# Where two kinds of weight stores stand in the transfers' queue, in a kernel of windowed attention and a Fourier-mixed feed-forward layer

## The chip, the cores and the metric

The kernel runs on one core of a Trainium2 chip. Such a core has TensorE (PE; the profile shows its weight loads apart as PEld), VectorE (DVE), ScalarE (ACT), GpSimd (POOL) and SyncE (SP). Each engine works through its own instructions in order, and SP does nothing here but issue transfers between the off-chip memory (DRAM) and on-chip memory. A transfer that has to wait for data or for a buffer holds SP until it can go, and with it all transfers that stand behind. The metric is the device time of one execution in microseconds (us); several runs are taken and their median compared.

## What is computed

Two layers, one after the other, for 4 sequences of 768 positions.

```python
# attention: 8 heads of 64, a window of 128 positions and 4 sink positions
keep = is_sink | in_window
scores = np.where(keep, scale * q @ k.T, -1e9)
x = softmax(scores) @ v                       # (4, 768, 512)
# Fourier mixing and feed-forward
u = x + real(fft(fft(x, axis=1), axis=2))
un = (u - mean(u)) / sqrt(var(u) + 1e-6)
out = u + relu(un @ w_ch1) @ w_ch2            # w_ch1 512 x 2048, w_ch2 2048 x 512
```

The weights arrive as 64-bit floating point numbers, two 32-bit words each, and everything is computed to the accuracy of 32-bit numbers, though products run on TensorE with rounded operands: each operand is split into a rounded high part and a low part, and three products (high by high, high by low, low by high) are added up.

## The kernel before

**Stages.** The 24 blocks of 128 positions form six groups of four (`groups`). Attention and the Fourier mixing run first, up to about 205 us. Then comes the feed-forward layer of group 0, in which the weights are also converted; it ends at about 333 us with the first product of group 1. Groups 1 to 5 use the converted weights; from line 1375 on, under `tc.manual_schedule()`, the order of the instructions is the written one. Before that line, and so in group 0's stage, the compiler's scheduler decides the order on each engine: it goes by the order of the program, but takes later work where an instruction would have to wait.

**The raw weights.** w1 (w_ch1) and w2 (w_ch2) come in 16 slices each. `W_ORDER` interleaves them: for each pair p of slices, places 4p and 4p+1 are two slices of w1, 4p+2 and 4p+3 two of w2, so there are 32 loads, numbered 0 to 31. `load_w(i)` issues load i (L599, 512 KB) into a tile with the tag "ld" that has three buffers (`LDB`). `convert(i)` turns the two words of each number into one 32-bit number by three DVE instructions (L614, L615, L616), then calls `load_w(i + 3)`, whose load needs the buffer that has just been read.

**The split.** A converted slice goes through an ACT cast for the high part and a POOL subtraction for the low part: L625 and L626 for w1, into one half of `w_ring` (two halves, one for each pair in turn), L639 and L640 for w2, into tiles that stay. PE needs both: `ch1` (L676) multiplies by w_ring, `ch2` (L1172) by the w2 tiles.

**The stores.** Later groups need w1 again, and with it sums and differences of its quarters, as they use a product scheme with seven instead of eight half-size products. So for each pair p two things are written to `w_dram[p]` in DRAM:

- the quarters (L629, 768 KB): three of the four in w_ring, issued in `convert(4p + 1)` after the POOL subtraction L626;
- the sums (L661, 1024 KB): `combine_w1(p)` forms four sums on POOL (L651 to L654) in a tile `tq`; the inner function `halves`, put off to the next slice by the list `late`, splits them by ACT casts (L659) and POOL subtractions (L660) into the tile `to`, and stores it. `tq` and `to` have one buffer each.

**The loop.** For each slice f of group 0 the loop at L1316 runs `ch1`, the relu (`split`, L1165 and L1166, tile h_sb), `ch2` of the slice before, the conversions of places 2f+4 and 2f+5, the `late` work and `combine_w1`. In the last slices it also prepares group 1 (`prepare_1`: L551, L552, L560, L1230, and the sums of the activations L1268, L1271, L1274). After the loop the tiles for the later stream of weights are set up: three of them take the buffers of the raw loads ("ld"), others those of `to`, `tq` and h_sb, and `load(n)` (L1364) reads `w_dram` back into them as w_c, w_t, w_q and w_h.

Of the kernel before, what the change touches and what calls it, by code (L numbers as in the profile page):

```python
# [205 lines left out]
def kernel(  # L206
# [14 lines left out]
    nc = tc.nc  # L221
    V, A, G, T = nc.vector, nc.scalar, nc.gpsimd, nc.tensor

    def f32(ap):
        return ap.bitcast(F32)
# [10 lines left out]
    w_dram = [dpool.tile([P, 7, 512], F32, name=f"wd{i}") for i in range(NPR)]  # L236
# [37 lines left out]
    def run(general):  # L274
        tag = "g" if general else ""
        with ExitStack() as p1:
# [314 lines left out]

            W_ORDER = [(w, 2 * p + j) for p in range(NPR) for w in range(2) for j in range(2)]

            def load_w(i):
                if i < 2 * NF:
                    which, f = W_ORDER[i]
                    r = npool.tile([P, 512, 2], I32, tag="ld", name=f"raw{i}", bufs=LDB)
                    src = w1i[f].rearrange("p c f -> p (c f)") if which == 0 else w2i[P * f:P * f + P]
                    nc.sync.dma_start(r.rearrange("p f t -> p (f t)"), src)  # L599
                    raw[i] = r  # L600

            def convert(i, pool=None):

                which, f = W_ORDER[i]
                r = raw.pop(i)
                if which == 0:
                    if f % 2 == 0:
                        state["tw"] = npool.tile([P, 2, 512], I32, tag="tw", name=f"tw{f}", bufs=1 if general else 2)
                    t = state["tw"][:, f % 2]
                else:  # L610
                    t = npool.tile([P, 512], I32, tag="qs0", name=f"cv{i}", bufs=QSB)

                w = state["h"].tile([P, 512], I32, tag="cw", name=f"cw{i}")
                V.tensor_scalar(w, r[:, :, 1], 3, 0x3FFFFFF8, op0=ALU.logical_shift_left, op1=ALU.bitwise_and)  # L614
                V.scalar_tensor_tensor(w, r[:, :, 1], -0x40000000, w, op0=ALU.bitwise_and, op1=ALU.bitwise_or)  # L615
                V.scalar_tensor_tensor(t, r[:, :, 0], 29, w, op0=ALU.logical_shift_right, op1=ALU.bitwise_or)  # L616
                load_w(i + LDB)
                tf = t.bitcast(F32)
                if which == 0:
                    if f == 0:  # L620
                        state["ring"] = npool.tile([P, 2, 4, 2, 256], F32R, tag="ring", name="w_ring", bufs=1)
                    fb = state["ring"][:, f // 2 % 2]
                    d = [fb[:, 0:2, j] if f % 2 == 0 else fb[:, 3:1:-1, j] for j in range(2)]
                    tf = tf.rearrange("p (h c) -> p h c", h=2)
                    A.copy(d[0], tf)  # L625
                    G.tensor_tensor(d[1], tf, f32(d[0]), op=ALU.subtract)  # L626
                    Wt[f, 0] = [[d[j][:, cc // 2, P * (cc % 2):P * (cc % 2) + P] for cc in range(NCC)] for j in range(2)]
                    if f % 2 == 1:
                        nc.sync.dma_start(w_dram[f // 2][:, 0:3], f32(fb[:, 0:3]).rearrange("p k s c -> p k (s c)"))  # L629
                        state["t", f // 2] = state["tw"].bitcast(F32)  # L630
                    return
                if NWA <= f < NWA + NHALF:

                    if f == NWA:
                        state["fold"] = [npool.tile([P, NHALF, DM], F32R, tag=t, name=f"w_{t}", bufs=1) for t in ("gh", "gl")]
                    d = [t[:, f - NWA] for t in state["fold"]]
                else:
                    d = [pool.tile([P, 512], F32R, name=f"w{f}_{j}") for j in range(2)]
                A.copy(d[0], tf)  # L639
                G.tensor_tensor(d[1], tf, f32(d[0]), op=ALU.subtract)  # L640
                Wt[f, 1] = d
# [3 lines left out]
            def combine_w1(p, pool):  # L645

                t = state.pop(("t", p))
                b11, b21, b12, b22 = t[:, 0, :256], t[:, 0, 256:], t[:, 1, :256], t[:, 1, 256:]
                q = pool.tile([P, 4, 256], F32, tag="tq", name=f"tq{p}")
                o = pool.tile([P, 4, 2, 256], F32R, tag="to", name=f"to{p}")  # L650
                G.tensor_tensor(q[:, 1], b12, b11, op=ALU.subtract)  # L651
                G.tensor_tensor(q[:, 0], b22, q[:, 1], op=ALU.subtract)
                G.tensor_tensor(q[:, 2], b22, b12, op=ALU.subtract)
                G.tensor_tensor(q[:, 3], b21, q[:, 0], op=ALU.subtract)  # L654

                def halves():
                    for j in (0, 2):
                        with tc.issue_after(state["relu"]):
                            A.copy(o[:, j:j + 2, 0], q[:, j:j + 2])  # L659
                        G.tensor_tensor(o[:, j:j + 2, 1], q[:, j:j + 2], f32(o[:, j:j + 2, 0]), op=ALU.subtract)  # L660
                    nc.sync.dma_start(w_dram[p][:, 3:7], f32(o).rearrange("p k s c -> p k (s c)"))  # L661

                late.append(halves)

# [15 lines left out]
            def start_ffn(s):  # L680
                state["h"] = p1.enter_context(tc.tile_pool(name="ps_h" + tag, bufs=1, space=PSUM))
                banks.append((p1.enter_context(tc.tile_pool(name="ps_n" + tag, bufs=1, space=PSUM)), "n", 1))
                for i in range(LDB):
                    load_w(i)
                for i in range(2):
                    at(s + CONV_AT[i], "V", lambda i=i: convert(i))
                for f in range(2):
                    at(s + CH1_AT[f], "T", lambda f=f: hp.append(ch1(0, f, unT0)))
# [458 lines left out]
            if general:  # L1147
# [4 lines left out]
                s = 0  # L1152
# [4 lines left out]
            else:  # L1157
                s = window_attention(fourier, load_constants)
# [155 lines left out]
            for i in (2, 3):  # L1314
                convert(i, wa)
            for f in range(NF):  # L1316
                ps = hp.pop(0) if f < 2 else ch1(0, f, unT0)
                hs[f] = g0.tile([P, 2, 512], F32R, tag="h", name=f"h_sb{f}", bufs=2)
                hs[f] = [hs[f][:, i] for i in range(2)]
                split(hs[f], ps)  # L1320
                if pw is None:
                    do(1)
                if f > 0:
                    ch2(f - 1, hs.pop(f - 1), po)
                for i in range(2 * f + 4, min(2 * f + 6, 2 * NF)):
                    if i % 2 and pw is None:
                        do(1)
                    if W_ORDER[i][0] == 1 and W_ORDER[i][1] == NWA + NHALF and pw is None:
                        while ev:
                            do(1)  # L1330
                        pf.close()
                        pf = None
                        pw = p1.enter_context(tc.tile_pool(name="wb" + tag, bufs=1))
                        state["x"] = [pw.tile([P, 7, 512], F32R, name=f"x{i}") for i in range(2)]
                        state["xf"] = pw.tile([P, 2, NCC, 256], F32, name="xf")
                    convert(i, wa if pw is None else pw)
                while late:
                    late.pop()()
                if f == 0 or f % 2 == 1 and f // 2 + 1 < NPR:
                    combine_w1((f + 1) // 2, g0)  # L1340
                if f == PREP:
                    steps = prepare_1()
                for _ in range(PREP_N if f >= PREP else 0):
                    next(steps, None)
            for _ in steps:
                pass
            while late:
                late.pop()()

            places = [npool.tile([P, 2, 2, 256], F32R, tag="ld", name=f"w1_c{i}", bufs=LDB) for i in range(LDB)]  # L1350

# [23 lines left out]
            with tc.manual_schedule():  # L1375
# [101 lines left out]
                for it in range(NIT):  # L1477
# [12 lines left out]
                    for k in range(7):  # L1490
                        if BANK.index(BANK[k]) == k:
                            pool, t = {"B": banks[it % 2][:2]}.get(BANK[k], (state["h"], {"A": "h", "C": "cw"}.get(BANK[k])))
# [4 lines left out]
                        a, b, c = (ps.get(x) for x in "ABC")  # L1497
# [102 lines left out]
                for g in range(2, len(groups)):  # L1600
# [7 lines left out]
                    ps, t, uh = {}, 0, {}  # L1608
                    for it in range(0, NIT, 2):
                        for k in range(7):  # L1610
                            for i in range(2):
                                c = it + i
# [4 lines left out]
                                p = ps[i, BANK[k]]  # L1617
# [37 lines left out]
                    for s2 in range(7 * NIT):  # L1655
                        k, c = divmod(s2, NIT)
                        if c == 0 and BANK.index(BANK[k]) == k:
                            ps[BANK[k]] = get(2, BANK[k], f"q{BANK[k]}_{g}")
                        p = ps[BANK[k]]
# [16 lines left out]
                        if g == 2 and 6 <= s2 < 6 + NPR:  # L1676
                            f = s2 - 6
                            for a in range(2):
                                nc.sync.dma_start(f32(Wt[2 * f, 1][a])[:, 256:], t_dram[f][:, 3, 256 * a:256 * a + 256])
                        do_x(xs, s2)  # L1680

    run(False)
    general = nc.values_load(outside[0:1, 0:1])
    with tc.If(general != 0):
        run(True)
# [77 lines left out]
```

## Time and profile before

| | us |
|---|---|
| median of 3 runs | 750.85 |
| lowest and highest run | 748.47, 751.24 |
| profiled execution, its own time | 752.84 |
| span of the profile, first to last instruction | 751.0 |
| PE busy in the span | 719.0 (96%) |
| DVE busy | 558.1 (74%) |
| ACT busy | 357.2 (48%) |
| POOL busy | 272.7 (36%), all of it before 430 us |
| mean granted TensorE clock | 0.988 |

The profile shows one execution. A row of instructions gives its start and duration, the engine, the line, the operation, the tiles it writes and reads, how many are merged into the row, and in square brackets how long the engine was idle before and what ended that. A row of waits gives who waited for whom, the total in us, how often, and the longest. Transfers appear at SP's issue; the time until the data has landed is listed apart.

### The profile page before, as it was taken

To read this page: it belongs to the slowest core of one execution; us is meant where nothing else is said; L and a number is where in the kernel's file an instruction comes from. 1 tells how busy PE (TensorE), PEld (TensorE's weight loads), DVE (VectorE), ACT (ScalarE), POOL (GpSimd) and SP (SyncE) were. 2 spreads that over 40 slices of the span, in tenths; PEclk is the share of its full clock that TensorE was granted. 3 is DMA by queue.
4 is the path that set the end of the run, shared out by engine and by line. 5 is a ranking of instruction groups with operands and counts; after the bars stand their busy time and mean duration, and the time that the engine had idled before them with its cause. 6 is when DMAs were issued, how large, how long until landed. Compare 5 with 4: busy or idle time off the path is not lost.

```text
span 751.0 us, 15699 instructions
## 1 busy us (share of the span) xinstructions
PE 719.0 (96%) x5539; PEld 644.0 (86%) x5539; DVE 558.1 (74%) x1299; ACT 357.2 (48%) x901; POOL 272.7 (36%) x391
## 2 busy tenths in 40 slices
PE   7999998999989999998999999999999999999996
PEld 5676876867868887687899999999999999999996
DVE  6678578888799888958677666957697578846772
ACT  4687666676633537423324144533444245523541
POOL 2467367478466898842995000000000000000000
PEclk9899999999999999999999999999999999999998
DMA  9754624533225898889999798879975897759831
GB/s 298 243 166 132 172 72 140 163 114 103 72 71 179 298 342 306 284 306 404 344 311 326 243 348 304 292 242 385 370 245 177 295 396 256 258 211 371 277 98 61
DMA packets 109576, 181.69 MB, mean 242 GB/s; under 512 B 9868, under 2 KB 44812, under 8 KB 108336
## 3 DMA queue, kind: packets, MB, share of 16 engines
q1 hardware_dynamic: 109200, 176.83, 69.2%
q0 software_dynamic: 288, 3.76, 1.3%
q8 instruction: 46, 0.75, 0.4%
q14 instruction: 42, 0.34, 0.1%
HBM read 148.04 MB, written 32.51 MB: 240 GB/s over the span
## 4 chain that ended last, share of the span: by engine, by line
PE 67%; DVE 14%; POOL 7%; issue 4%; ACT 4%; DMA 2%; SPq 1%; DVEq 0%; POOLq 0%; ACTq 0%
PE pB L1391 10%; PE qB L1568 9%; PE pA L1391 7%; PE pC L1391 6%; PE qC L1568 6%; PE qA L1568 6%; PE o L1419 5%; PE xt L854 4%; PE s L759 4%; PE pt L816 2%; PE za L398 1%; PE zb L398 1%; DVE sm L778 1%; POOL w_ring L626 1%; PE h L676 1%
## 5 line engine op out<-in xcount | busy, mean ns | idle before, releaser
L1590 ACT CAST hring<-x 128x512 fp32r<-128x512 f32 x92 | 57.0, 619 | 52.0 <-PE qB L1568 18.8
L784 ACT ACTIVATE sm<-sm,mx 128x132 f32<-128x132 f32 x192 | 75.9, 400 | 5.5 <-DVE mx L778 5.5
L1594 DVE TENSOR_TENSOR hring<-x,hring 128x512 fp32r<-128x512 f32 x92 | 63.4, 689 | 14.8 <-ACT hring L1590 9.6
L759 PE MATMUL s<-ring,q 64*128 64x260 f32 x320 | 50.8, 424 | 7.7 <-DVE mx L778 4.6
L778 DVE CUSTOM_DVE_ANT_0 sm<-s,mask 128x132 f32<-128x132 f32 x192 | 48.5, 293 | 7.1 <-PE s L757 1.7
L676 PE MATMUL h<-un_slots,w_ring 128*128 128x512 f32 x192 | 49.4, 404 | 2.1 <-POOL w_ring L626 1.5
L676 PEld LDWEIGHTS h<-un_slots,w_ring 128*128 128x128 f32 x192 | 36.3, 194 | 10.7 <-POOL w_ring L626 2.6
L759 PEld LDWEIGHTS s<-ring,q 64*128 64x128 f32 x320 | 27.9, 191 | 20.5 <-issue 6.7
L823 ACT COPY pta<-pt 128x512 f32<-128x512 f32 x48 | 28.1, 585 | 26.5 <-PE pt L816 26.4
L854 PE MATMUL xt<-ptl,ldv 128*64 128x128 f32 x384 | 40.2, 291 | 0.0
L1568 PE MATMUL qA<-w,hring 128*128 128x256 f32 x312 | 39.8, 279 | 0.0
L1419 PE MATMUL o<-w,hring 128*128 128x512 f32 x156 | 38.5, 393 | 1.3 <-ACT hring L1165 1.1
L1172 PE MATMUL o<-w,h_sb 128*128 128x512 f32 x156 | 38.3, 393 | 0.5 <-POOL w L640 0.5
L1568 PEld LDWEIGHTS qA<-w,hring 128*128 128x128 f32 x312 | 37.9, 189 | 0.0
L765 DVE COPY_PREDICATED s<-older,s 128x256 f32<-128x256 uint8 x80 | 33.7, 421 | 4.7 <-PE s L759 4.6
L784 ACT ACTIVATION_READ_ACCUMULATOR sm<-sm,mx 128x1 f32 x192 | 36.7, 191 | 0.0
L854 PEld LDWEIGHTS xt<-ptl,ldv 128*64 128x64 f32 x384 | 22.7, 139 | 15.2 <-issue 5.2
L832 POOL TENSOR_SCALAR_AFFINE_SELECT ptl<-pta 128x512 f32<-128x512 f32 x48 | 31.4, 654 | 11.6 <-ACT pta L823 11.6
L1568 PE MATMUL qB<-w_c,hring 128*128 128x256 f32 x288 | 35.2, 281 | 0.0
L1419 PEld LDWEIGHTS o<-w,hring 128*128 128x128 f32 x156 | 28.5, 188 | 7.5 <-ACT hring L1165 1.3
L1172 PEld LDWEIGHTS o<-w,h_sb 128*128 128x128 f32 x156 | 28.9, 188 | 7.0 <-POOL w L640 0.9
L1568 PEld LDWEIGHTS qB<-w_c,hring 128*128 128x128 f32 x288 | 34.5, 189 | 0.0
(296 smaller groups left out, 1961.8 us busy)
## 6 DMA issues: line engine op xcount, KB each, us to landing
w_c<-wd SPq DMA_DIRECT2D x96, 256.0 KB, 4.8
w_h<-wd SPq DMA_DIRECT2D x76, 256.0 KB, 5.0
w_t<-wd SPq DMA_DIRECT2D x70, 256.0 KB, 4.9
raw<-in_moe_w_ch_dram SPq DMA_DIRECT2D x32, 512.0 KB, 4.9
w_c<-td SPq DMA_DIRECT2D x48, 256.0 KB, 4.5
w_q<-wd SPq DMA_DIRECT2D x38, 256.0 KB, 5.0
wd<-to SPq DMA_DIRECT2D x8, 1024.0 KB, 6.1
ldv<-in_v_dram SPq DMA_DIRECT2D x28, 256.0 KB, 3.0
```

What stands on the lines that cost most here:

```text
L676: T.matmul(ps[:, :tb], a[cc], x[:, :, cc, :], start=n == 0, stop=n == 3 * NCC - 1)
L759: T.matmul(ps[:, j, :P + W], st["q", g][rows, hp, :], keys(g, 2 * hp + j), start=True, stop=True)
L765: V.copy_predicated(ps[:, :, P + NS:P + W], older[qi > 2], ps[:, :, 0:P])
L778: V.tensor_tensor_reduce(sm[:, h % 4], ps[:, j, P:P + W], mask[min(qi, 3)], -SCALE, 3.0e38, ALU.add, ALU.min, accum_out=mx[:, 0, h:h + 1])
L784: A.activation(sm[:, h % 4], sm[:, h % 4], AF.Exp, bias=mx[:, 0, h:h + 1], scale=-1.0, accum_out=mx[:, 1, h:h + 1])
L854: T.matmul(ps[D * j:D * j + D, p, :], st["v", kb(g) - i][:, h, :], a[:, h % 4, :], start=i == 0, stop=i == n - 1)
L1172: T.matmul(po[i], a[:, P * i:P * i + P], x, start=f == 0 and n == 0, stop=f == NF - 1 and n == 2)
L1391: T.matmul(ps[:, 256 * j:256 * j + 256], w[:, j, a, cs], x[:, xs], start=BANK.index(BANK[k]) == k and j == c == m == 0, stop=j == c == 1 a ...
L1419: T.matmul(po[i], h[:, a, j, ts_], x, start=first and j == m == 0, stop=last and j == 1 and m == 2)
L1568: T.matmul(ps[:, 256 * t:256 * t + 256], h[:, a, j, P * t:P * t + P], x, start=BANK.index(BANK[k]) == k and c == t == j == m == 0, stop=c ...
L1590: A.copy(hi, x)
L1594: V.tensor_tensor(*args, op=ALU.subtract)
```

## The change

`store_after(i, fn)` is new: it calls `fn`, which issues a store, inside `tc.issue_after(loads[i])`, so that the store comes behind load i in SP's queue. If load i has not been issued by the program yet, the store is kept in `stores` and called right after that load in `load_w`. A store kept for a load that never comes (i of 32 and more) is called after the loop.

```diff
+            stores, loads = {}, {}
+
+            def store_after(i, fn):
+                if i in loads:
+                    with tc.issue_after(loads[i]):
+                        fn()
+                else:
+                    stores.setdefault(i, []).append(fn)
+
             def load_w(i):
...
-                    nc.sync.dma_start(r.rearrange("p f t -> p (f t)"), src)
+                    ld = nc.sync.dma_start(r.rearrange("p f t -> p (f t)"), src).ins
                     raw[i] = r
+                    loads[i] = ld
+                    for fn in stores.pop(i, ()):
+                        store_after(i, fn)
...
-                        nc.sync.dma_start(w_dram[f // 2][:, 0:3], f32(fb[:, 0:3]).rearrange("p k s c -> p k (s c)"))
+                        store_after(2 * f + 4, lambda: nc.sync.dma_start(
+                            w_dram[f // 2][:, 0:3], f32(fb[:, 0:3]).rearrange("p k s c -> p k (s c)")))
...
-                    nc.sync.dma_start(w_dram[p][:, 3:7], f32(o).rearrange("p k s c -> p k (s c)"))
+                    store_after(4 * p + 8, lambda: nc.sync.dma_start(
+                        w_dram[p][:, 3:7], f32(o).rearrange("p k s c -> p k (s c)")))
...
             while late:
                 late.pop()()
+            for i in sorted(stores):
+                for fn in stores.pop(i):
+                    fn()
```

The quarters of pair p are stored for an odd slice f = 2p + 1, so 2f + 4 is load 4p + 6. For the sums it is load 4p + 8. Nothing else changes: the same transfers, buffers and computations.

## The prediction

> **What bounds the kernel now.** I read three stretches first (busy time by engine; PE is TensorE's matmuls, PEld its weight loads), to see whether the engine that does most of the work has any room where the moved stores are issued. These are the first feed-forward group's stages: raw weights come in, VectorE (DVE) converts them, ScalarE (ACT) and GpSimd (POOL) split them, the stores go out.
>
> ```profile
> core 0: us, PE busy (x) PEld busy (x) DVE busy (x) ACT busy (x) POOL busy (x), PEclk, DMA share, GB/s
> 205.00:235.00 30.00, 25.82 (x168) 21.83 (x167) 28.35 (x51) 10.57 (x22) 16.13 (x17) 0.94 0.28 89
> 235.00:285.00 50.00, 50.00 (x246) 42.54 (x246) 44.85 (x82) 21.31 (x40) 45.58 (x47) 1.00 0.87 309
> 285.00:333.00 48.00, 44.70 (x198) 34.78 (x196) 36.75 (x54) 24.59 (x43) 38.12 (x34) 1.00 0.82 285
> ```
>
> From 235 to 285 us the matmuls leave no gap at all: 50.00 of 50.00. A load that comes earlier there has nothing to shorten. From 205 to 235 DVE is the full one (28.35 of 30), and only a few loads are issued. So what can be won lies from 285 to 333, where PE is idle for 48.00 - 44.70 = 3.3 us. The waits of PE in that stretch say on whom (total, times, longest):
>
> ```profile
> PE h L676 <- POOL w_ring L626: 1.5, 2, 0.9
> PE unt L560 <- ACT un L552: 1.1, 1, 1.1
> PE o L1172 <- POOL w L640: 0.5, 1, 0.5
> PE pA L1391 <- DMA w_c<-wd: 0.4, 1, 0.4
> ```
>
> Three of these four rows (1.5 + 0.5 + 0.4 = 2.4 us) can depend on stores and loads; the 1.1 us are the next group's normalization. Now the transfers' queue (SP) and the consumer of its loads, from 205 to 334 us:
>
> ```profile
> SPq L629 <- POOL w_ring L626: 31.7, 8, 5.4
> SPq L661 <- POOL to L660: 20.3, 7, 4.8
> ```
>
> ```profile
> DVE cw L614 <- DMA raw<-in_moe_w_ch_dram: 7.9, 7, 2.6
> ```
>
> Here is the point of the change. SP issues in order, and the stores of w1's quarters (L629) and sums (L661) hold it for 52 us in all, waiting for POOL. Yet DVE waited only 7.9 us for raw weights: mostly SP would have waited for a free buffer anyway. The price is 7.9 us at the very most on DVE, and far less on PE.
>
> **The change part by part.** Its instructions are the same, 8 + 8 stores and 32 loads, at the same issue cost; only their order on SP changes. In the new rule the quarter store of pair p goes behind load 4p+6, the sums store behind load 4p+8; where there is no such load, both go after the loop. The late part of the queue as it runs now:
>
> ```profile
> 298.06 0.33 SPq L629 DMA_DIRECT2D wd<-w_ring  x1
> 298.49 3.56 SPq L599 DMA_DIRECT2D raw<-in_moe_w_ch_dram  x3
> 302.29 0.33 SPq L661 DMA_DIRECT2D wd<-to  x1
> 307.59 0.33 SPq L599 DMA_DIRECT2D raw<-in_moe_w_ch_dram  x1
> 311.93 0.33 SPq L629 DMA_DIRECT2D wd<-w_ring  x1
> 312.34 2.59 SPq L599 DMA_DIRECT2D raw<-in_moe_w_ch_dram  x2
> 315.59 0.33 SPq L661 DMA_DIRECT2D wd<-to  x1
> 317.25 0.33 SPq L599 DMA_DIRECT2D raw<-in_moe_w_ch_dram  x1
> 323.00 0.33 SPq L629 DMA_DIRECT2D wd<-w_ring  x1
> 327.46 0.33 SPq L661 DMA_DIRECT2D wd<-to  x1
> 327.88 4.03 SPq L1364 DMA_DIRECT2D w_c<-wd  x6
> ```
>
> Counted back from load 31 (317.25): loads 29 and 30 at 312.34, 28 at 307.59, 25 to 27 from 298.49. So the quarters of pair 5 (298.06) move behind load 26, its sums (302.29) behind load 28, the quarters of pair 6 (311.93) behind load 30, its sums (315.59) behind load 31. Pair 7's two stores stay last, ahead of the loads w_c of the next stage. Next, DVE and ACT, at the places where such a load was late:
>
> ```profile
> 290.08 0.69 DVE L614 TENSOR_SCALAR cw<-raw 128x512 int32<-128x512 int32 x1 [2.58 <-DMA raw<-in_moe_w_ch_dram]
> ...
> 291.58 0.69 DVE L1166 SCALAR_TENSOR_TENSOR h_sb<-h,h_sb 128x512 fp32r<-128x512 f32 x1
> ...
> 303.43 0.69 DVE L614 TENSOR_SCALAR cw<-raw 128x512 int32<-128x512 int32 x1 [0.62 <-DMA raw<-in_moe_w_ch_dram]
> ```
>
> ```profile
> 290.95 0.59 ACT L1165 ACTIVATE h_sb<-h 128x512 fp32r<-128x512 f32 x1
> ...
> 310.70 0.62 ACT L659 CAST to<-tq 128x512 fp32r<-128x512 f32 x1 [1.98 <-POOL tq L652]
> 313.09 0.62 ACT L659 CAST to<-tq 128x512 fp32r<-128x512 f32 x1 [1.77 <-POOL tq L654]
> 313.62 0.61 ACT L639 CAST w<-cv 128x512 fp32r<-128x512 f32 x1
> ```
>
> **Term 1, load 25: -0.62 us.** It was issued at 298.49, right behind the store that had waited for POOL; without that store it arrives earlier, and DVE's 0.62 us at 303.43 go. The bounds are 0 (DVE's gain is eaten by its own later work) and -0.9 (the longest wait of PE for w_ring); I take DVE's row, since DVE, ACT and POOL feed PE's next wait in line.
>
> **Term 2, load 21: 0.** The longest wait, 2.58 us at 290.08, looks best and is worth least: the quarters of pair 4 move from ahead of that load to behind the next one, but two instructions later DVE stands in line at 291.58 behind ACT's h_sb, which ends at 290.95 + 0.59 = 291.54. With that order DVE gains 0.04 us. Only if the order also changes does anything come through, at most what PE's rows have left: 2.4 - 0.62 = 1.8. Bounds -1.8 and 0; I take 0.
>
> **Term 3, the sums' one buffer: +0.4.** The tile the sums are stored from (to) has one buffer, so pair 6's casts (310.70) cannot write it before pair 5's store has landed. The landing times (KB each, median us from issue):
>
> ```profile
> raw<-in_moe_w_ch_dram SPq DMA_DIRECT2D x28, 512.0 KB, 4.9
> wd<-to SPq DMA_DIRECT2D x8, 1024.0 KB, 6.1
> wd<-w_ring SPq DMA_DIRECT2D x8, 768.0 KB, 4.0
> ```
>
> Now that store goes at 302.29 and lands by 308.4, well before 310.70. Behind load 28 (307.59, or 306.97 with term 1) it goes at 307.3 to 308.0 and lands at 313.4 to 314.1: the casts are 2.7 to 3.4 us late. What stands behind them:
>
> ```profile
> 310.63 1.27 POOL L626 TENSOR_TENSOR w_ring<-tw,w_ring 128x512 fp32r<-128x512 f32 x1
> ...
> 313.01 2.55 POOL L660 TENSOR_TENSOR to<-tq,to 128x512 fp32r<-128x512 f32 x2
> 315.52 2.52 POOL L640 TENSOR_TENSOR w<-cv,w 128x512 fp32r<-128x512 f32 x2
> ```
>
> In the order of now, the w cast (313.62) and POOL's w (315.52), for which PE already waits 0.5 us, come behind them. Casts at 313.4 end POOL's two sums at 313.4 + 0.62 + 2.55 = 316.6 instead of 315.56: 1.1 us later, 1.8 from a landing at 314.1. But this stretch is ordered by the compiler's scheduler (in program order where it can, other work where an instruction would wait), not by hand; if it puts the sums' casts behind the w cast, the cost is nothing and PE's 0.5 us go. Bounds -0.5 and +1.8. I take +0.4, nearer to the middle of 0 and 1.1 than to either end.
>
> The Trainium skill ("DMA: Bandwidth & Descriptors", Anatomy of one DMA) fits one transfer as about 2.0 us plus bytes over 436 GB/s, so 1 MB lands after an estimated 4.4 us, and by it this term would shrink by 1.7 us. The trace, 6.1 us for the same thing, does not agree, and its number is used.
>
> The quarters need no such term: w_ring has two halves, so a store that is two loads later still has a whole pair's time against 4.0 us of landing.
>
> **Term 4, the end: 0.** The sums of pair 6 go at 317.7 instead of 315.59 (behind load 31, and not before term 3's 316.6), land at 323.8, and pair 7's cast and two POOL sums take 0.62 + 2.55 more: 327.0, against 327.46 now. A landing 0.6 late or one w of 1.26 between the sums gives up to 328.9. The loads w_c stand behind pair 7's store and PE waits 0.4 for them, so the bounds are -0.4 and +1.4; I take 0.
>
> The sum is -0.62 + 0 + 0.4 + 0 = -0.2 us. The profiled execution took 752.84, its span 751.0 and 1.84 around it; it becomes 752.6. The median, 750.85, is 1.99 below that execution, so the **forecast is 750.6 us**: no change that can be measured (about 0.5%, 3.75 us, is what a measurement of this kernel tells from none).
>
> **The rivals.** *Fast:* the loads come early enough that all of PE's waits that hang on them go, 2.4 us: 748.4; with the 1.1 us of the normalization, which a new order could also move, 747.3. For it: SP's 52 us. Against it: term 2, and that a freed 0.62 us is all I find on the path.
>
> *The full stretch is not full:* if PE had room from 235 to 285 us, the other waits of DVE for raw weights, 7.9 - 2.58 - 0.62 = 4.7 us, could come through too, at most: 745.9. Against it: no gap in 50 us. The Trainium skill ("Perfetto Trace Analysis", Identifying the Most-Contended Engine) calls matmul busy time a poor measure and wants the weight loads' share, 42.54 of 50.00 here; by that rule there is room. The trace of before cannot settle it; I give it 4 in 100.
>
> *Slow, by the one buffer:* terms 3 and 4 at their ends, 1.8 + 1.4 = 3.2 us, with nothing back from term 1: 754.1; if the stores land at 6.7 rather than 6.1, twice 0.6 more, 755.3. It decides from the point where pair 5's store lands after 310.70, which by the numbers above it does; only the order on ACT saves it. *Nothing moves:* SP waits for the same buffers in the new order, 750.85; this is not told from the forecast.
>
> **How the numbers follow.** Forecast or nothing 0.58, fast 0.16, not full 0.04, slow 0.22. Below 747.1 (0.5% faster) ends half of the not-full rival and about half of the fast one: 0.10. Above 754.6 ends two thirds of the slow one: 0.15. Within lies 0.75. Range: from 747.6 (the fast rival but for its end) to 754.8 (the slow one with one late landing), which leaves some 0.2 outside.
>
> **What would show it.** In the changed trace the wait of DVE for raw weights falls well below 7.9 us, SP's wait at L629 falls too, and the load that now goes at 298.49 comes ahead of the quarters. PE's waits from 285 to 333 show term 1; a cast L659 that waits for a transfer wd<-to shows term 3, and the time of the first w_c load against 327.88 term 4. I am wrong if the order of ACT or POOL changes in a way that opens a gap on PE before 285 us, or if PE's 50.00 shrink there.

## The result, and the profile after

The changed kernel takes **754.84 us** (median of 9 runs, 754.03 to 760.83) against 749.89 for the kernel before (9 runs, 748.47 to 752.07) beside it: ratio **1.0081**, 95% interval 1.0062 to 1.0100. It is slower by some 5 us; the forecast was 750.6. The profiled execution of after took 754.41, its span is 752.6. One of the twelve executions of e9 below took 1362.52 us at a mean granted clock of 0.949 and is not counted in its ratio.

The lines shift in after: L599 is now L610 (raw load), L626 L640 and L629 L643 (w_ring, its store), L640 L655 (w of w2), L659, L660 and L661 are L674, L675 and L676 (cast, subtraction and store of the sums), L676 L692 (product h), L1166 L1182 (h_sb), L1364 L1383 (loads w_c and on), L1391 L1410 (the products pA, pB, pC of the next stage). In most kernels of the experiments these differ by a few lines again.

The two executions ran their first 100 us at different granted clocks (0.95 before, 1.00 after), so their times are compared from a common mark: the product zb just ahead of the stage that waits 0.25 us for DVE. A time of after plus 2.97 (203.58 - 200.61) stands on before's clock. The timeline of PE of before, at the mark and then at the next stage's first products:

```profile
203.58 0.62 PE L398 MATMUL zb<-cst,gh 128*128 128x386 f32 x2 [0.25 <-DVE zb L413]
...
333.14 1.68 PE L1391 MATMUL pA<-x,w_c 128*128 128x256 f32 x12 [0.44 <-DMA w_c<-wd]
334.65 1.58 PE L1391 MATMUL pB<-x,w_c 128*128 128x256 f32 x12
336.08 1.58 PE L1391 MATMUL pC<-x,w_c 128*128 128x256 f32 x12
337.50 1.58 PE L1391 MATMUL pA<-x,w_t 128*128 128x256 f32 x12
```

The same of after:

```profile
200.61 0.63 PE L398 MATMUL zb<-cst,gh 128*128 128x386 f32 x2 [0.24 <-DVE zb L413]
...
318.83 2.60 PE L692 MATMUL h<-un_slots,w_ring 128*128 128x512 f32 x10 [1.96 <-POOL w_ring L640]
...
331.13 1.58 PE L1410 MATMUL pA<-x,w_c 128*128 128x256 f32 x12
335.32 2.78 PE L1410 MATMUL pB<-x,w_c 128*128 128x256 f32 x12 [2.61 <-DMA w_c<-wd]
337.90 2.05 PE L1410 MATMUL pC<-x,w_c 128*128 128x256 f32 x12
339.78 1.57 PE L1410 MATMUL pA<-x,w_t 128*128 128x256 f32 x12
```

From the mark to the first product pA: 129.56 us before, 130.52 after, so the whole stage has cost 0.96. (In before, 0.44 of it is a wait for w_c; in after pA has none, so up to that wait the stage costs 1.4.) To the first product with w_t: 133.92 before, 139.17 after, 5.25 later. So **4.29 us are lost within three products**, and the rows account for them: a wait of 2.61 for a load w_c, then a pB that takes 2.78 instead of 1.58 and a pC of 2.05 instead of 1.58, as the granted clock has dropped (0.54 during pB, a row below, and 0.78 from 338.1 to 340.0 us): 2.61 + 1.20 + 0.47 = 4.28. The rest of the span adds nothing (from the mark to the end, 547.42 and 551.99: 4.57 later).

The waits of after, of DVE, ACT, POOL and SP from 205 to 334 us (total, times, longest; the fence ends with PE's from 285 to 340):

```profile
DVE h_sb L1182 <- ACT h_sb L1181: 8.9, 7, 2.5
...
DVE cw L628 <- DMA raw<-in_moe_w_ch_dram: 0.6, 2, 0.4
...
ACT h_sb L1181 <- PE h L692: 12.8, 8, 3.5
...
ACT to L674 <- DMA wd<-to: 2.2, 2, 1.4
...
POOL w L655 <- ACT w L654: 12.8, 6, 4.8
...
SPq L610 <- DVE tw L630: 31.8, 11, 5.1
SPq L610 <- DVE cv L630: 26.2, 10, 3.4
...
SPq L676 <- POOL to L675: 7.9, 3, 5.7
SPq L643 <- POOL w_ring L640: 4.2, 1, 4.2
...
PE h L692 <- POOL w_ring L640: 3.2, 3, 2.0
PE pB L1410 <- DMA w_c<-wd: 2.6, 1, 2.6
```

Three rows of before that answer to these:

```profile
DVE h_sb L1166 <- ACT h_sb L1165: 3.5, 5, 1.2
...
ACT h_sb L1165 <- PE h L676: 8.5, 6, 3.5
...
POOL w L640 <- ACT w L639: 6.1, 4, 4.8
```

The change does what it says. SP's 52 us of waiting for POOL at the stores are 12.1 in the same two rows, and DVE's 7.9 us of waiting for raw weights are 0.6. SP now waits for free buffers instead (L610), as the loads stand in front. But DVE got little for it: its wait in line behind ACT's h_sb rose by 5.4, and ACT's h_sb in turn waits for PE's own product h (8.5 us before, 12.8 after), so that this line ends at PE. PE's waits for w_ring from POOL went from 1.5 to 3.2 us. And POOL now stands idle for 12.8 us at w, where it stood 6.1 (in both, one early wait makes 4.8 of it). The busy times of after, in the columns that the prediction shows; the first two stretches are those of the prediction set on after's clock, 235 to 285 and 285 to 333 us of before:

```profile
232.03:282.03 50.00, 49.09 (x240) 41.14 (x238) 45.69 (x79) 21.36 (x39) 43.81 (x46) 1.00 0.85 303
282.03:330.03 48.00, 44.31 (x196) 34.74 (x197) 37.40 (x54) 24.29 (x43) 38.19 (x34) 1.00 0.80 280
335.30:338.10 2.80, 2.78 (x13) 2.78 (x14) 0.00 (x0) 0.00 (x0) 0.00 (x0) 0.54 1.06 407
```

In the stretch that was full, DVE does 0.8 us more and POOL 1.8 us less than before: the conversions are ahead, the splits behind. PE's 50.00 have become 49.09 through a gap of 0.86 us at its end, in which PE waits for POOL's w (L655). Now the end of SP's queue in after:

```profile
315.23 0.33 SPq L610 DMA_DIRECT2D raw<-in_moe_w_ch_dram  x1
317.57 0.33 SPq L676 DMA_DIRECT2D wd<-to  x1
322.15 0.33 SPq L643 DMA_DIRECT2D wd<-w_ring  x1
322.56 1.35 SPq L1383 DMA_DIRECT2D w_c<-wd  x2
329.64 0.32 SPq L676 DMA_DIRECT2D wd<-to  x1
330.06 2.94 SPq L1383 DMA_DIRECT2D w_c<-wd  x4
```

Pair 7's store of the sums goes 129.03 us after the mark; in before it was 327.46 - 203.58 = 123.88. It is 5.15 late. Two loads w_c have slipped in ahead of it, and the third, which pB needs, stands behind it from 322.56 + 1.35 = 323.9 to 330.06. Pair 6's store is late already, 317.57 - 200.61 = 116.96 us after the mark against 112.01: 4.95. What led to that begins with pair 5. Three rows of after, of POOL, SP and ACT (its splits, its store, and the casts of pair 6):

```profile
299.07 3.14 POOL L675 TENSOR_TENSOR to<-tq,to 128x512 fp32r<-128x512 f32 x2 [0.28 <-ACT to L674]
306.41 0.43 SPq L676 DMA_DIRECT2D wd<-to  x1
313.56 1.14 ACT L674 CAST to<-tq 128x512 fp32r<-128x512 f32 x2
```

Pair 5's splits end at 302.21, but its store goes only at 306.41, behind load 28, where the change has put it: 4.2 us later. In before the store (302.29) followed the splits at once. With 6.7 us of landing (the median of these stores in after) the tile is free at some 313.1, and pair 6's casts follow at 313.56, its splits from 315.00 to 317.54. On POOL they now stand just ahead of the w_ring of slice 14, for which PE waits 1.96 us (row 318.83); in before it waited 0.59 for that slice.

The end of POOL's work in before:

```profile
323.63 1.30 POOL L660 TENSOR_TENSOR to<-tq,to 128x512 fp32r<-128x512 f32 x1
324.89 1.29 POOL L640 TENSOR_TENSOR w<-cv,w 128x512 fp32r<-128x512 f32 x1
326.13 1.30 POOL L660 TENSOR_TENSOR to<-tq,to 128x512 fp32r<-128x512 f32 x1
328.10 1.30 POOL L640 TENSOR_TENSOR w<-cv,w 128x512 fp32r<-128x512 f32 x1 [0.67 <-ACT w L639]
```

And in after:

```profile
322.76 1.31 POOL L655 TENSOR_TENSOR w<-cv,w 128x512 fp32r<-128x512 f32 x1
325.70 1.30 POOL L655 TENSOR_TENSOR w<-cv,w 128x512 fp32r<-128x512 f32 x1 [1.63 <-ACT w L654]
327.06 2.55 POOL L675 TENSOR_TENSOR to<-tq,to 128x512 fp32r<-128x512 f32 x2
```

Before, the two splits of the sums (`to`) lie between and ahead of the two w, and fill POOL's time while a w waits for its cast. After, both come last, and POOL idles 1.63 us at w though the sums in `tq` are formed by then. ACT's casts of this pair, at 326.37, wait for no transfer in the trace: the order, which the compiler's scheduler sets here, has put them last. Pair 6's store (317.57) lands at some 324.3, so with the one tile another order could have brought them forward by some 2 us, an estimate, and not by the whole 5.15.

**Theory:** the tile `to` has one buffer. With the store of pair p-1 later in the queue the tile is free later, so the scheduler orders pair p's splits behind other work, in the last pair behind everything; its store holds the loads of the next stage. **Rivals:** the late store is only the accident of its place ahead of the loads w_c (the tile has no part); or POOL is simply too full, as the loads come earlier.

### The profile page after: what moved, and what is told of

Same layout as the page of the kernel before. It is cut to its first block, busy times and chain, and to the rows that moved or that the text cites. A ratio compares the mean times of both kernels' runs of the same rounds, so it can differ in the third digit from the quotient of the medians.

```text
span 752.6 us, 15696 instructions
## 1 busy us (share of the span) xinstructions
PE 718.2 (95%) x5539; PEld 643.5 (86%) x5539; DVE 561.8 (75%) x1299; ACT 357.0 (47%) x901; POOL 271.3 (36%) x391
## 4 chain that ended last, share of the span: by engine, by line
PE 49%; DVE 4%; issue 1%; ACT 1%; DMA 0%; SPq 0%; DVEq 0%
PE pB L1410 10%; PE qB L1587 9%; PE pA L1410 7%; PE pC L1410 6%; PE qC L1587 6%; PE qA L1587 6%; PE o L1438 5%; DVE bn L519 1%; PE unt L560 1%; DVE hring L1182 0%; DVE x L1646 0%; DMA w_c<-wd 0%; DVE x L1649 0%; DVE un L554 0%; DVE stat L520 0%
## 5 line engine op out<-in xcount | busy, mean ns | idle before, releaser
L775 PE MATMUL s<-ring,q 64*128 64x260 f32 x320 | 49.2, 411 | 7.5 <-DVE mx L794 3.4
L692 PE MATMUL h<-un_slots,w_ring 128*128 128x512 f32 x192 | 49.5, 402 | 3.9 <-POOL w_ring L640 3.2
L692 PEld LDWEIGHTS h<-un_slots,w_ring 128*128 128x128 f32 x192 | 35.7, 192 | 13.7 <-POOL w_ring L640 5.0
```

The lines of the kernel that those rows point to most:

```text
L692: T.matmul(ps[:, :tb], a[cc], x[:, :, cc, :], start=n == 0, stop=n == 3 * NCC - 1)
L775: T.matmul(ps[:, j, :P + W], st["q", g][rows, hp, :], keys(g, 2 * hp + j), start=True, stop=True)
```

## The experiments

Ratios are to the kernel before beside the run, with 95% intervals; 5 us are 0.67%.

### The end of the stage

**e1** takes pair 7's store out of the way: it is called behind the loads w_c.

```diff
-            for i in sorted(stores):
+            for i in sorted(stores)[:-1]:
...
             for n in range(NWS - 1):
                 load(n)
+            for fn in stores.pop(max(stores)):
+                fn()
```

> The changed kernel with one thing different: the store of pair 7's sums is called after the loads of the next stage, so that all six loads w_c go ahead of it on SP; the orders on ACT, POOL and DVE stay those of the changed kernel. Theory A (the loss is made at the end: the last sums are cast last, their store at 329.64 holds the loads w_c): PE, which is only 1.0 us late where the first product of group 1 starts and 4.8 us late two products later, gets these 3.8 us back, about 751. Theory B (the loss is made in the stage, by the order of sums and weights on POOL, and the end only shows it): 754.8, as the changed kernel. Theory C (the end, but through the buffer: w_t takes the place of the sums' tile and cannot be loaded before the store has landed, so the wait moves from the loads w_c to w_t, the fourth product): PE waits there until about 338.1 instead of going on at 339.8, 753.1.

Measured: 756.61 us, 1.0082 (1.0053 to 1.0111): nothing gained. Of the theories, C names the wait that came, though its 753.1 is 3.5 too low (1.5 of it are the ten products of the last section's first row). PE's waits in e1:

```profile
PE pA L1412 <- DMA w_t<-wd: 5.9, 1, 5.9
```

The wait for w_c is gone and a longer one for w_t has taken its place. SP's queue in e1:

```profile
332.12 0.42 SPq L676 DMA_DIRECT2D wd<-to  x1
...
339.27 1.75 SPq L1383 DMA_DIRECT2D w_t<-wd  x4
```

The tile w_t has the tag "to", so it takes over the buffer of the sums, and its load goes 7.15 us behind their store, about a landing time (6.7 us) later. The tile ties the end together twice, by the queue and by its buffer.

**e2** is e1 with the places in another order, so that w_t is first needed by the sixth product and not by the fourth.

```diff
-            places += [w1_t[:, 0], w1_t[:, 1], g0.tile(..., name="w1_q")]
+            w1_q = g0.tile(..., name="w1_q")
             places.append(g0.tile(..., name="w1_h0", bufs=2))
+            places += [w1_q, w1_t[:, 0], w1_t[:, 1]]
```

> As e1_wc_first, and the places of the next stage's weights in another order: w_h and w_q are the fourth and fifth, the two that lie in the sums' tile (w_t) the sixth and seventh. Theory A: nothing more than e1. Theory B: 754.8. Theory C: both holds at the end are gone, about 751, and e1 above it by some 2 us.

Measured: 751.94 us, 1.0020 (0.9999 to 1.0042), and no wait of PE for w_c or w_t is left. So by the medians the end carries 0.6 of the 0.8%. **e4**, the same end (e2's lines and the one below) in the kernel before, tells whether that is a gain of its own.

```diff
+                    store = lambda: nc.sync.dma_start(w_dram[p][:, 3:7], ...)
+                    store_after(4 * p + 8, store) if p == NPR - 1 else store()
```

> The kernel of before with the end of e2: pair 7's sums are stored after the loads w_c, w_h and w_q, and w_t comes sixth and seventh. PE waited 0.4 us for w_c at the end of the stage, so 0.4 us at most can be won by that wait: 749.5 by all theories. If more is won, the end holds PE before too, in a wait that the profile of before gives to another name.

Measured: 749.95 us, 0.9992 (0.9975 to 1.0009). It is not: e2 repairs what the change broke.

**e3** goes the other way: kernel before, with only the last pair's splits put behind everything, as after has them, and the loads w_c 2 to 6 behind their store.

```diff
-                while late:
+                while late and f < NF - 2:
...
-            for n in range(NWS - 1):
-                load(n)
+            load(0)
+            with tc.issue_after(state["store"]):
+                for n in range(1, NWS - 1):
+                    load(n)
```

> The kernel of before with nothing moved in the stage: only pair 7's sums are split after the loop, and all loads w_c but the first weight's two go behind their store, as in the changed kernel. Theories A and C (the end alone makes the loss): about 4 us over before, 753 to 755. Theory B: as before, 750, at most 1 us over it.

Measured: 753.57 us, 1.0035 (1.0015 to 1.0054), as theories A and C expected. PE's waits in e3:

```profile
PE pB L1393 <- DMA w_c<-wd: 2.6, 1, 2.6
```

One wait of 2.6 us costs 753.57 - 750.77 = 2.8 us. This order at the end, with the loads behind the store, makes some 40% of the loss by itself; here the products behind the wait took 1.69 and 1.58 us, so the clock's 1.67 us of after are not in it.

### One kind of store at a time

**e5** moves only the stores of the quarters, **e6** only those of the sums.

```diff
 e5 (after)
-                    store_after(4 * p + 8, lambda: nc.sync.dma_start(w_dram[p][:, 3:7], ...))
+                    nc.sync.dma_start(w_dram[p][:, 3:7], ...)
 e6 (after)
-                        store_after(2 * f + 4, lambda: nc.sync.dma_start(w_dram[f // 2][:, 0:3], ...))
+                        nc.sync.dma_start(w_dram[f // 2][:, 0:3], ...)
```

> Only the quarters' stores are put behind later loads; the sums' stores have no rule. Theory D (the earlier loads let the scheduler put the weights' conversions ahead of the sums' splits everywhere, so that the sums fall behind whether or not their own stores are moved): the last splits stand last on POOL here too, and the store stands ahead of the loads w_c, so the time is that of the changed kernel, 754 to 756. Theory E (the sums' stores, moved behind loads, hold the sums' one tile): nothing of the loss, 750 to 751.

> Only the sums' stores are moved; the quarters' keep their place. Theory E: the whole loss, 754 to 756. Theory D: part of it; one split and one weight of 1.3 us each stand in the other order at the end of POOL, so the last store goes some 1.3 us earlier than in the changed kernel, 752 to 754.

Measured: e5 754.96 us, 1.0054 (1.0040 to 1.0068); e6 **764.59 us, 1.0190** (1.0173 to 1.0206). The parts don't add up to the whole: 0.54 and 1.90% alone, 0.81 together. Neither theory holds as written: e5 lies where D has it, E's values are missed in both, and D's in e6. In e5 the splits of pair 7 come last on POOL too, though no store of sums was moved by a rule. But they go later there all the same, pair 5's 107.6 us after its mark (200.78) against 98.7 in before and pair 6's 118.8 against 112.0, and one cast waits 2.8 us for wd<-to. Most of e5's loss is in the stage and not at its end: its first product pA comes 3.95 us later than before's, with waits of PE of 3.2 us for the normalization (1.1 before) and 3.4 for w_ring (1.5). In e6 the buffer shows itself at run time. ACT's timeline of e6:

```profile
275.69 0.62 ACT L673 CAST to<-tq 128x512 fp32r<-128x512 f32 x1 [7.27 <-DMA wd<-to]
```

And SP's, where pair 2's store goes:

```profile
268.92 0.32 SPq L643 DMA_DIRECT2D wd<-w_ring  x1
269.30 0.42 SPq L675 DMA_DIRECT2D wd<-to  x1
```

Pair 3's cast stands 7.27 us for the store of pair 2's sums, issued at 269.30 and landed 6.4 later. It could not go before 269.30, as the store of the next quarters, left in place, stood ahead of it in the queue and waited for POOL. So the two kinds are not independent: sums moved past quarters inherit their wait.

### Is POOL full?

By its busy time it is not: from 285 us on POOL works 38.19 of 48 us in after and 38.12 in before. What is left is whether single orders make the 1 us of the stage that e2 keeps. Both runs are e2 with one order changed: **e7** puts POOL's subtraction for the sums of pair 6 behind the w_ring of load 28, for which PE waited; **e8** puts DVE's sums of group 1's activations behind conversion 24.

```diff
 e7
+                        with tc.issue_after(state["g", 28 if p == 6 else 0]):
                             G.tensor_tensor(o[:, j:j + 2, 1], ...)
 e8
+                        with tc.issue_after(state["c", 24]):
                             do_x(xs_1, k)
```

> e2_places_after with one swap on POOL: the two splits of pair 6's sums (2.5 us) go behind the low part of slice 14's w1 instead of ahead of it. All other orders stay. If PE's longest wait in the stage, 1.95 us for that low part, is the splits' doing, it falls to some 0.6 us and the time from 751.9 to about 750.6. If PE waits there for slices whose conversions are late on VectorE, the wait stays and the time stays within 0.4 us of 751.9.

> e2_places_after with the first sums of group 1's activations put behind conversion 24 on VectorE, as they nearly stood before; the scheduler then orders what follows anew. If VectorE's order made the waits of PE at 302 to 310 us (0.6 + 0.6 + 0.6 us), these go and the time falls by 1 to 1.9 us, to 750 to 751. If POOL's order makes the loss of the stage, nothing changes: 751.9.

Measured: e7 751.93 us, 1.0016 (0.9998 to 1.0033); e8 752.21 us, 1.0029 (1.0012 to 1.0047), against 1.0020 in e2. In e7 the wait of 1.95 us for w_ring became 0.40 and the next slice's became 1.30, so the splits were the cause of that wait, but the time stayed; in e8 one of 2.6 came up. Inside the stage the waits change places, and neither exchange won its 1 us.

### The tile

**e9** is the direct test: kernel after, and the sums of pairs 4 and 6 get a second tile, made of slots of the activations' tiles that are unused at that time. As its halves lie apart, the store of every pair is cut in two transfers.

```diff
-                o = pool.tile([P, 4, 2, 256], F32R, tag="to", name=f"to{p}")
+                if p in (4, 6):
+                    o = [t[:, 5:7].rearrange("p k (a c) -> p (k a) c", a=2) for t in state["x"]]
+                else:
+                    o = pool.tile([P, 4, 2, 256], F32R, tag="to", name=f"to{p}")
+                    o = [o[:, :, i] for i in range(2)]
...
+                def store():
+                    for i in range(2):
+                        nc.sync.dma_start(w_dram[p][:, 3:7, 256 * i:256 * i + 256], f32(o[i]))
...
-                    store_after(4 * p + 8, lambda: nc.sync.dma_start(...))
+                    store_after(4 * p + 8, store)
```

> Kernel after, with a second tile for the sums of pairs 4 and 6 (unused slots of the activations' tiles, their store cut in two DMAs), so that the casts of pairs 5, 6 and 7 wait for the store of two pairs before instead of one. One-buffer theory (the late store of pair p-1 holds the only tile, which delays the splits of the sums, puts pair 7's last of all, and with them the store that stands ahead of the loads w_c): ACT's 2.2 us of waiting for wd<-to goes, pair 7's store is issued 4 to 5 us earlier, PE's 2.6 us wait for w_c goes, and 750 to 751.5 us. Rival (the loads come earlier and the splits fall behind because POOL is full, the tile has no part in it): 754 to 755.5 us, with pair 7's store where it was.

Measured: **750.44 us, 0.9998** (0.9980 to 1.0017). The whole loss is gone, with every store where the change put it. The end of POOL's work in e9:

```profile
319.55 1.29 POOL L683 TENSOR_TENSOR to<-tq,to 128x512 fp32r<-128x512 f32 x1
320.81 1.28 POOL L655 TENSOR_TENSOR w<-cv,w 128x512 fp32r<-128x512 f32 x1
322.06 1.28 POOL L683 TENSOR_TENSOR to<-tq,to 128x512 fp32r<-128x512 f32 x1
323.31 1.29 POOL L655 TENSOR_TENSOR w<-cv,w 128x512 fp32r<-128x512 f32 x1
```

The splits lie between the w again. SP's queue of e9 behind them:

```profile
320.37 3.36 SPq L677 DMA_DIRECT2D wd<-to  x2
323.82 3.19 SPq L1390 DMA_DIRECT2D w_c<-wd  x6
```

The loads w_c follow in one piece, and PE waits for none of them. PE's waits for POOL's w_ring are 1.6 us (3.2 in after, 1.5 before), so the loss in the stage is gone too. One point of the expectation was missed: ACT still waits 1.7 us for wd<-to (2.2 in after), in the pairs before the fourth, where the second tile does not reach.

**e15** and **e16** are the kernels after and before with the cut store and one tile; **e11** is before with the second tile, cut store included; **e10** is e9 with the end of e2.

```diff
 e15, e16
                 o = pool.tile([P, 4, 2, 256], F32R, tag="to", name=f"to{p}")
+                o = [o[:, :, i] for i in range(2)]
 (and the store in two transfers, as in e9)
```

> Kernel after with one tile for the sums as it is, and only their store cut in two DMAs as in e9. One-buffer theory: the cut does not free the tile, the casts still wait and pair 7's store comes as late: 754 to 757 us. Rival (it was the two shorter DMAs that helped in e9): 750 to 752 us.

> Kernel before with only the sums' store cut in two DMAs. If e11's +0.35% came from the cut: 752.5 to 754 us. If it came from the second tile (another order of the splits): 749.5 to 751 us.

> Control: kernel before with the same second tile and its two DMAs for pairs 4 and 6, nothing moved. One-buffer theory: the profile of before shows no wait of a cast for the store, so within 0.5 us of before (749.5 to 750.5 us). If the second tile or the cut DMAs have an effect of their own, it shows here and is to be taken off e9.

> Run e9 with the end of run e2 (pair 7's store behind the loads w_c, the places of the fourth product's loads swapped). One-buffer theory: the end is whole in e9 already, so this adds nothing: 750 to 751.5 us, within 0.5 us of e9. If instead the end and the tile are two separate costs: 749 to 750, below e9 and e2. Rival (tile has no part): as e2, 752 us.

Measured: e15 756.3 us, 1.0084 (1.0058 to 1.0110); e16 751.71, 1.0022 (1.0007 to 1.0038); e11 753.28, 1.0035 (1.0020 to 1.0051); e10 751.43, 1.0015 (0.9996 to 1.0033). By e15 the cut transfers do not help: it is the tile. By e10, which gains nothing (it lies 1.0 us above e9 where 0.5 was expected; the intervals overlap), the end is whole in e9 already. e11 is a miss: the second tile is not neutral in the kernel before but costs 0.35%. e16 shows that the cut alone costs 0.22%, between the two ranges that its expectation names, so it can be most of that, but the intervals overlap.

**e14** and **e13** add the tile to e5 and e6.

> Kernel e5 (only the quarters' stores moved) with the second tile of e9. One-buffer theory: e5's cast that waited 2.8 us for wd<-to and PE's 1.3 us wait for w_c go: 749 to 752 us, against 755.0 in e5. If the second tile by itself costs 3 us with no store of the sums moved, as in e11: 753 to 755.

> Kernel e6 (only the sums' stores moved) with the second tile of e9. One-buffer theory: the 7.3 us wait of a cast for wd<-to goes, and with it most of e6's 14.5 us: 750 to 754 us. Rival (with the quarters' stores left where they were, the later sums' stores stand behind two waits for POOL, and the tile has little part in the loss): 758 to 765 us.

Measured: e14 749.90 us, 0.9999 (0.9985 to 1.0013), where e5 had 1.0054, and PE's 3.2 us for the normalization are 0.3, its 3.4 for w_ring 1.2; e13 **767.06 us, 1.0219** (1.0196 to 1.0243), where e6 had 1.0190. e13 is a plain miss. ACT's timeline of e13 shows one reason:

```profile
279.74 0.62 ACT L681 CAST to<-tq 128x512 fp32r<-128x512 f32 x1 [7.80 <-DMA wd<-to]
```

This is pair 3 again, still with the one tile: the expectation overlooked that the long wait of e6 comes before the first pair that has the second one. So e13 does not test the theory where e6 loses most. What the rest of e13's 16.5 us comes from is open. All kernels of this kind, as ratios:

| stores moved | one tile | one tile, cut store | two tiles, cut store |
|---|---|---|---|
| none | 1 | 1.0022 | 1.0035 |
| quarters | 1.0054 | not run | 0.9999 |
| sums | 1.0190 | not run | 1.0219 |
| both | 1.0081 | 1.0084 | 0.9998 |

Wherever the quarters' stores are moved, the second tile takes the loss away; where they stay, it does not. Even with nothing moved late, the cut and the second tile change the scheduler's order and cost 0.22 and 0.35%, so differences of that size say little. The two that the tile takes away, 0.86 (e15 to e9) and 0.55% (e5 to e14), are larger; the second includes the cut of the store.

### Only the last stores

**e12** is the kernel before with the sums' stores of pairs 5, 6 and 7 alone moved.

```diff
+                    store = lambda: nc.sync.dma_start(w_dram[p][:, 3:7], ...)
+                    store_after(4 * p + 8, store) if p >= 5 else store()
```

> Kernel before with only the stores of the sums of pairs 5, 6 and 7 behind later loads (the quarters' and the first five sums' stores where they were). One-buffer theory: the delay needs only the last stores; the casts of pairs 6 and 7 wait for wd<-to, pair 7's splits come last and its store holds w_c: 752 to 754.5 us. Rival (the backlog builds up over the whole stage from earlier moved stores): 750 to 751 us.

Measured: 753.82 us, 1.0041 (1.0023 to 1.0058), in the range of the one-buffer theory. But not all of its picture: a cast waits 3.0 us for wd<-to, yet in this order one split w follows the last sums, and PE has no wait for w_c. The profiled execution of e12, 759.16, lies 5.3 above its median, so its times are not read further.

## Why the prediction was wrong

- **Term 1 (-0.62) and term 2 (0).** The waits of DVE that they are about did go, 7.9 to 0.6 us. Nothing of it reached PE: the first product pA came 0.96 later. Most of DVE's time went into the line behind ACT's h_sb (3.5 to 8.9), which itself stands behind PE; term 2 had seen such a line at 291.58, term 1 had only a bound for it. Only with the second tile do the moved stores look worth something: e9 at 0.9998 lies 0.37% below its control e11, though it is no faster than the kernel before.
- **Term 3 (+0.4) is the step that failed.** Its working had two branches: the casts wait and the w comes late (+1.1 to +1.8), or "if it puts the sums' casts behind the w cast, the cost is nothing". The scheduler took the second branch, and that one was priced wrong. On before's clock, pair 5's store goes at 309.38, where the term had 307.3 to 308.0, and pair 6's splits end at 320.51 against 315.56. What then stands behind them is the w_ring of slice 14, which the term left out (PE's wait 1.96 instead of 0.59). Behind the w casts the splits no longer fill POOL's waits for w (6.1 to 12.8 us), and in the last pair they are last of all. e3 shows that this order at the end, with the loads w_c behind the store, costs 2.8 us in the kernel before. e9 and e15 show that the tile, and not the transfers' places as such, brings the loss about. (The fit of the Trainium skill that stands beside this term is given on its page for transfers issued through GpSimd, and SP issues these; it has no part in the sum.)
- **Term 4 (0, bounds -0.4 and +1.4)** took over the error: it set out from pair 6's store at 317.7, and that went at 320.54 on before's clock. It also let pair 7's splits start as soon as the tile was free, so that its store came at 327.0 to 328.9; it went at 332.61, 5.15 later than in before. Two things were not in the term: PE's clock, 1.67 us behind the wait, and the buffer that w_t takes over, because of which moving the store alone (e1) does not help. The term measures 4.29.
- **The sum.** +0.96 in the stage and +4.29 at the end make 5.25 where -0.2 stood; the medians say 754.84 - 749.89 = 4.95.
- **Rivals.** The slow one, by the one buffer, was right in its mechanism, and at 0.22 it had too little chance. Its 754.1 to 755.3 hold the measured 754.84, but in part by luck: it is made of 1.8 us in the stage and 1.4 at the end, where 0.96 and 4.29 were measured, 1.67 of these from a clock that it did not have. Its sentence "only the order on ACT saves it" has it the wrong way round: that order is how the buffer's cost came in. Of the others nothing was seen: PE's 50.00 in the full stretch became 49.09, a loss. That, and the gap of 0.86 us by POOL's order, is what the prediction had named as its own sign of being wrong.

**Open:** why the second tile and the cut cost 0.35% in the kernel before; what makes e13 as slow as it is beyond pair 3; why e9 and e14, with all loads early, end level with the kernel before. In the profile e9 reaches its first product with w_t at 332.56, 1.2 us sooner after its mark (199.88) than before does, and has nothing left of it at the end. None of the versions beats the kernel before.

## What to carry to other kernels

Before a store is moved back in a queue, ask who next writes its source tile: with one buffer, the store's landing is the date on which the next round may begin. Here the scheduler put that round's work behind other work, so that hardly a wait for the store showed in the trace: compare the order of the instructions on each engine, too. Follow the last round in particular, and what the buffer becomes afterwards, since nothing of the same kind comes later that could hide it. And a wait that vanishes on an engine off the path (7.3 us here) is no gain until PE's own row shows it.

## What the chip showed that was not expected

A gap on PE can cost more than its length, and not always the same. In after, the ten products behind a gap of 1.96 us took 2.60 (row 318.83 above). PE's row of e1, at the same place behind the same gap:

```profile
317.93 4.14 PE L692 MATMUL h<-un_slots,w_ring 128*128 128x512 f32 x10 [1.96 <-POOL w_ring L640]
```

And of e11:

```profile
310.32 3.61 PE L684 MATMUL h<-un_slots,w_ring 128*128 128x512 f32 x10 [1.98 <-POOL w_ring L626]
```

Of seven such gaps of 1.95 to 2.14 us ahead of ten products h, five left the products at 2.56 to 2.60 us and two, these rows, did not (1.5 and 1.0 us more; granted clock 0.57 in e1 from 318 to 322 us, 0.68 in e11 from 310.3 to 313.9). In e13 a gap of 1.74 us, shortly behind one of 0.55, cost 1.4 more. Behind the 2.61 us gap of after it was 1.67, behind 2.56 in e8 1.4, behind 2.59 in e3 0.1. So the price of a gap of about 2 us ranges from its own length to nearly twice that. The Trainium skill ("TensorE: Matmul & The Clock Gate", Part 1: The HAM clock gate) has the clock halved after an idle window of some 3.4 us, and says that the window runs freely, without regard to when work starts. That the same gap fares differently agrees with a free-running window; that 1.96 us can be enough is less than the page's figure, and no run here shows the windows themselves.

Two stores of different kinds in one queue are no independent edits: e5 and e6 cost 0.54 and 1.90%, the two together 0.81.
